# mLSTM, mixture of experts and feed-forward in one kernel: who makes the low parts of w2, how q is laid out, and when x and the first weights arrive

## The chip, the core and the metric

The kernel runs on one core of a Trainium2 chip. The metric is the device time of one execution in microseconds (us): the median of three runs.

## The reference

Three stages follow one another. The first runs over 768 steps, the second sends every token to one of eight experts, the third is a feed-forward net with a PReLU.

```python
for t in range(S):                       # 2 batches x 8 heads, S = 768, head size 40
    m_new = np.maximum(f_gate[:, :, t] + m, i_gate[:, :, t])
    ...
    C = f_stab * C + i_stab * einsum('bhd,bhe->bhde', vt, kt)
    n = f_stab * n + i_stab * kt
    y[:, :, t] = sigmoid(o_gate) * (C @ qt) / max(|n . qt|, 1)
x = y as (1536 tokens, 320)
# experts: 8, capacity 384, 320 -> 1024 -> 320, top 1, weighted by the gate's probability
h = np.maximum(np.einsum('ecd,edf->ecf', disp, w1), 0.0)
out[i] = gate_w[i] * np.einsum('ecf,efd->ecd', h, w2)[expert_idx[i], pos[i]]
# feed-forward: 320 -> 2048 -> 320, weights given in float64
h = x @ w_in
y = (max(h, 0) + alpha * min(h, 0)) @ w_out
```

(Shortened, with the shapes as comments.)

## The kernel before, in words

**mLSTM.** The 1536 tokens are 12 chunks of 128, six for each batch, and line 715 loops over them. A chunk needs a decay matrix `Gb` (GpSimd sets its upper triangle, line 378; ScalarE takes its exponentials), scores of q against k on TensorE (line 393, its moving operand `qbd` is q laid out block-diagonally: three heads share 120 rows, and a head's own 40 rows stand in that head's columns, zeros elsewhere), their product with the decay on VectorE (`Pt`), values (line 456), the state's update (`Ups`, line 427, from `kw`, which GpSimd makes of `tk`, line 402), and a gated output (`rs` on GpSimd, line 492; `xt` on VectorE, line 499). Finished rows are scattered to `disp`, a table of expert slots in DRAM, by an indirect DMA from GpSimd (line 639). Inputs come two chunks at a time: `load_pair` (line 254) loads k and q (`qk`), the block-diagonal q by three DMAs into one of two `qbd` tiles (line 264), and values and keys with tokens as rows (`tk`, line 271). A table of numbers (line 97) says when the loads that don't belong to a chunk are issued: in chunks Z1 to Z1+3 the four quarters of expert 0's weights are loaded by `load_quarter` (line 177: w1 256 KB, its last rows 64 KB, w2 320 KB).

**Experts.** All products are in float32 with each operand split in a high and a low part. Layer 1 of an expert is eight steps f of 128 hidden columns, each eight matmuls of 256 slots (line 938); layer 2 for step f comes two steps later (`LAG`), three matmuls of 320 columns for each of two blocks of 128 slots (lines 950 to 952). A third block of slots runs only if it holds tokens (a run-time If, line 1169); here it does in two experts. Between the layers ScalarE makes `gh` (line 1072) and VectorE `gl` (line 1073). While expert e runs, the weights of expert e+1 are split into high and low parts, a half quarter a step: in even steps w1 (`split1`: ScalarE copies the high part `w1h`; VectorE makes the low part `w1l` and the last rows' low part, a 64x256 "shift" into `w1h`, line 188), in odd steps w2 (`split2`, line 222: ScalarE copies `w2h`, GpSimd makes `w2l`, 128x640). VectorE's part of `split1` is put on a list (`shifts`) that `low_rows` (line 190) empties in the next, odd step, behind that step's `gl` and x. The raw tile is then free and the load for expert e+2 goes out (line 1141). In three steps from XE on the next expert's x is transposed by TensorE and split. VectorE also converts a few tiles of the FFN's weights from float64 (`cv`, lines 976 to 981, five steps for each tile), as many steps as the tuple SC has at each f. When an expert's last accumulation is done, `finish` (line 1157) copies its two blocks, one on VectorE and one on ScalarE (line 1161), and stores them.

**FFN.** Four passes over quarters of the 2048 hidden columns; the first runs over four groups of 2, 2, 4 and 4 blocks of 128 tokens, the others over three groups of four blocks. A step has eight matmuls of 512 columns (layer 1), two passes of ScalarE (`ng`, `g`), VectorE's PReLU (line 1316), the split of g (`g3h` on ScalarE, `g3l` on VectorE, into one of three pairs `ghl3`), and layer 2 two steps later (line 1348). In the first pass the tokens of a group are transposed by TensorE (line 924) and split during the group before: the table XG gives the step for each of the three parts k; a group's layer 1 uses part 0, then part 2, then part 1. The tiles of the last group's x are named `w1h`, `w1l`, `w2h` and `w2l` like the expert tiles whose place they take.

**Order.** TensorE, ScalarE, VectorE and GpSimd run in the order in which the code is written; a queue stands still while its first instruction waits. The DMAs on SyncE's queue are put in order by the scheduler, and some are tied by `after` to an instruction (`anchor[i]`, the last of chunk i's `Pt`), so that they aren't issued ahead of it.

Of the kernel before, what the change touches and what calls it, by code (L numbers as in the profile page):

```python
# [53 lines left out]
def kernel(  # L54
# [177 lines left out]
    with ExitStack() as actx:  # L232
# [16 lines left out]
        for x in range(2):  # L249
            qbds.append(ap.tile([P, 3 * NG, PB], F32, tag=f"qbd{x}", name=f"qbd{x}"))  # L250
            nc.gpsimd.memset(qbds[x], 0.0)
        ins, sgs = {}, {}

        def load_pair(i2, anchor=None, late=None):
# [460 lines left out]
        for i in range(LB):  # L715
# [378 lines left out]
    def expert(e):  # L1094
# [200 lines left out]
    for np0, gi in [(0, g) for g in range(len(FIRST))] + [(p, g) for p in (1, 2, 3) for g in range(len(OTHERS))]:  # L1295
# [4 lines left out]
        for f in range(f0, f1):  # L1300
# [129 lines left out]
```

## Time and profile before

| | |
|---|---|
| median of three runs | 506.01 us (502.34, 506.01, 509.98) |
| profiled execution | 504.48 us, span 502.7 us |
| mean granted TensorE clock in it | 0.925 of full speed |
| busy: TensorE, VectorE, ScalarE, GpSimd | 454.7, 342.4, 246.3, 125.5 us |
| HBM read, written | 56.49 MB, 11.85 MB |

The profile is one execution. TensorE is busy 90% of the span, so what can be won lies in its gaps and in stretches at a lower granted clock. The 40 slices of the page put the slow ones (granted clock below nine tenths) in the mLSTM (to 125 us, with the routing that follows it), and single ones later; the experts run from about 125 to 303 us, the FFN to the end. "Idle before" names what ended an engine's wait; `DVEq` or `PEq` as a releaser is that engine's own sequencer, here at the branch of the If.

### The profile page before, as it was taken

To read this page: it belongs to the slowest core of one execution; us is meant where nothing else is said; L and a number is where in the kernel's file an instruction comes from. 1 tells how busy PE (TensorE), PEld (TensorE's weight loads), DVE (VectorE), ACT (ScalarE), POOL (GpSimd) and SP (SyncE) were. 2 spreads that over 40 slices of the span, in tenths; PEclk is the share of its full clock that TensorE was granted. 3 is DMA by queue.
4 is the path that set the end of the run, shared out by engine and by line. 5 is a ranking of instruction groups with operands and counts; after the bars stand their busy time and mean duration, and the time that the engine had idled before them with its cause. 6 is when DMAs were issued, how large, how long until landed. Compare 5 with 4: busy or idle time off the path is not lost. (4 is left out here: it accounts for less than half of the span.)

```text
span 502.7 us, 8039 instructions
## 1 busy us (share of the span) xinstructions
PE 454.7 (90%) x2800; PEld 408.0 (81%) x2800; DVE 342.4 (68%) x700; ACT 246.3 (49%) x558; POOL 125.5 (25%) x115
## 2 busy tenths in 40 slices
PE   5969998889879889796998898997999999999996
PEld 2658886787879889796998897895998898789995
DVE  7627683866788783859688224775889988764544
ACT  3446782525457544555556124562654454354442
POOL 4244325646534221423233224300000000000000
PEclk8759995966999999889899999997999999999999
DMA  6999999424786753657473003221221231000102
GB/s 190 263 278 337 351 317 253 147 78 133 241 254 197 222 175 88 212 155 244 147 220 94 22 1 103 74 84 42 73 59 53 57 101 52 2 0 1 52 20 86
DMA packets 42428, 68.86 MB, mean 137 GB/s; under 512 B 4383, under 2 KB 32354, under 8 KB 42383
## 3 DMA queue, kind: packets, MB, share of 16 engines
q1 hardware_dynamic: 41023, 64.18, 42.5%
q0 software_dynamic: 1152, 3.86, 2.4%
q8 instruction: 26, 0.43, 0.4%
q10 hardware_dynamic: 208, 0.24, 0.1%
q14 instruction: 19, 0.16, 0.1%
HBM read 56.49 MB, written 11.85 MB: 136 GB/s over the span
## 5 line engine op out<-in xcount | busy, mean ns | idle before, releaser
L188 POOL TENSOR_TENSOR w2l<-w2r,w2h 128x640 fp32r<-128x640 f32 x31 | 53.2, 1715 | 93.1 <-ACT w2h L224 77.8
L1316 DVE SCALAR_TENSOR_TENSOR g<-ng,nalt,g 128x512 f32<-128x512 f32 (+1 forms) x52 | 36.9, 709 | 47.5 <-ACT g L1315 47.4
L1314 ACT ACTIVATE ng<-hps 128x512 f32<-128x512 f32 (+1 forms) x52 | 29.4, 565 | 74.8 <-PE hps L938 73.3
L950 PE MATMUL acc<-w2h,gh 128*128 128x320 f32 x128 | 40.8, 319 | 4.9 <-DVEq L1169 4.9
L952 PE MATMUL acc<-w2h,gl 128*128 128x320 f32 x128 | 40.5, 316 | 1.6 <-DVE gl L1073 1.6
L951 PE MATMUL acc<-w2l,gh 128*128 128x320 f32 x128 | 40.4, 315 | 0.0
L1072 ACT ACTIVATE gh<-hps 128x256 fp32r<-128x256 f32 x50 | 19.1, 384 | 40.3 <-PE hps L938 38.5
L387 ACT ACTIVATE Gb<-Gb,bT 128x128 f32<-128x128 f32 x96 | 29.5, 388 | 12.3 <-POOL Gb L379 12.3
L188 DVE TENSOR_TENSOR w1h<-w1r,w1h 64x256 fp32r<-64x256 f32 x32 | 33.4, 1047 | 1.0
L188 DVE TENSOR_TENSOR g3l<-g,g3h 128x512 fp32r<-128x512 f32 (+1 forms) x52 | 33.5, 644 | 0.1
L1073 DVE SCALAR_TENSOR_TENSOR gl<-hps,gh 128x256 fp32r<-128x256 f32 x50 | 20.5, 421 | 18.6 <-ACT gh L1072 18.1
L952 PE MATMUL acc<-w2h,g3l 128*128 128x320 f32 x96 | 30.3, 316 | 2.4 <-DVE g3l L188 2.3
L952 PE MATMUL acc<-wouth,g3l 128*128 128x320 f32 x96 | 30.8, 321 | 0.3 <-DVE g3l L188 0.3
L950 PE MATMUL acc<-wouth,g3h 128*128 128x320 f32 x96 | 30.7, 320 | 0.1
L1319 ACT CAST g3h<-g 128x512 fp32r<-128x512 f32 (+1 forms) x52 | 30.6, 589 | 0.3 <-DVE g L1316 0.3
L951 PE MATMUL acc<-woutl,g3h 128*128 128x320 f32 x96 | 30.6, 319 | 0.0
L950 PE MATMUL acc<-w2h,g3h 128*128 128x320 f32 x96 | 29.8, 310 | 0.8 <-ACT g3h L1319 0.8
L456 PEld LDWEIGHTS Ops<-tk,Pt 128*128 128x128 f32 x192 | 26.7, 217 | 4.2 <-issue 2.6
L393 PE MATMUL qs<-qbd,qk 120*128 120x384 f32 (+1 forms) x72 | 30.1, 567 | 0.0
L951 PE MATMUL acc<-w2l,g3h 128*128 128x320 f32 x96 | 29.6, 309 | 0.0
L950 PEld LDWEIGHTS acc<-w2h,gh 128*128 128x128 f32 x128 | 25.1, 196 | 5.4 <-issue 3.8
L1315 ACT ACTIVATE g<-hps 128x512 f32<-128x512 f32 (+1 forms) x52 | 29.2, 561 | 0.0
(334 smaller groups left out, 1384.0 us busy)
## 6 DMA issues: line engine op xcount, KB each, us to landing
w2r<-w SPq DMA_DIRECT2D x32, 320.0 KB
w1r<-w SPq DMA_DIRECT2D x32, 256.0 KB
Gb<-gd SPq DMA_DIRECT2D x12, 512.0 KB
raw<-wout SPq DMA_DIRECT2D x8, 640.0 KB
raw<-win SPq DMA_DIRECT2D x8, 512.0 KB
tk<-tok SPq DMA_DIRECT2D x6, 648.0 KB
disp<-zt SPq DMA_DIRECT2D x4, 960.0 KB
qk<-qks SPq DMA_DIRECT2D x5, 720.0 KB
```

What stands on the lines that cost most here:

```text
L188: eng.tensor_tensor(out=out, in0=a, in1=b.bitcast(F32), op=ALU.subtract)
L387: nc.scalar.activation(Dt[i][:, h, :], Dt[i][:, h, :], AF.Exp, bias=bT[:, c, b * H + h:b * H + h + 1])
L393: nc.tensor.matmul(ps[:, :nh * P].rearrange("p (h t) -> p h t", h=nh), kst[:nh * D, g, :], qbd[:nh * D, h0:h0 + nh, :], start=True, stop=True,
L456: nc.tensor.matmul(Opss[i][:, h, :], Pts[i][:, h, :], v1t[:, h, :], start=True, stop=True)
L950: nc.tensor.matmul(a, gh[:, ms], wh, start=first, stop=False)
L951: nc.tensor.matmul(a, gh[:, ms], wl, start=False, stop=False)
L952: nc.tensor.matmul(a, gl[:, ms], wh, start=False, stop=last)
L1073: nc.vector.scalar_tensor_tensor(out=gl, in0=ps, scalar=0.0, in1=gh.bitcast(F32), op0=ALU.max, op1=ALU.subtract)
L1314: nc.scalar.activation(ng, ps, AF.Relu, scale=-1.0)
L1315: nc.scalar.activation(g, ps, AF.Relu)
L1316: nc.vector.scalar_tensor_tensor(out=g, in0=ng, scalar=nalt[:, f:f + 1], in1=g, op0=ALU.mult, op1=ALU.add)
L1319: nc.scalar.copy(gh, g)
```

## The change

**a.** In `split2` the low part of w2 can be made by VectorE, and in the experts always is: it goes on the list `shifts`, and `low_rows` now runs at every step, so that `w2l` stands in an even step and `w1l` with its shift in an odd one, behind the step's `gl` and x. Before, 28 of these ran on GpSimd in the experts, for experts 1 to 7.
**b.** The load that refills the raw quarter is issued one step later.
**c.** Both copies of `finish` go to ScalarE.
**d.** XE goes from 2 to 3, and the conversion steps of SC from f = 0, 5, 7 to f = 0, 2, 6.
**e.** For pairs 1 to 5 the block-diagonal q isn't loaded: `spread_q` makes it of `qk`, multiplying by a column `bd` that is one on a head's 40 rows and zero elsewhere: two products on GpSimd and one on ScalarE for each pair. The three DMAs of each of these pairs (320 KB) are gone, and the clearing of the second `qbd` tile.
**f.** Z1 goes from 6 to 7, and only two quarters of expert 0 are loaded in the loop over chunks, the other two behind it.
**g.** The x tiles `xq` become one slab, whose place is used in the FFN as a fourth pair of `ghl3`; layer 2 then follows three steps behind layer 1.
**h.** XG: the parts of the last group's x in the first pass are transposed at steps 0, 1, 2 instead of 1, 2, 3.

```diff
-    W1, W2, V7, V8, V9, NA, WA, WB, Z0, Z1, X0, LD, FL, XE, SC, SC0, F0, WC, LS, UO, DL, XG, LV, E0, S0, CUT = 12, 4, 0, (((0, 0, 0, 0), (1, 1, 1, 1), (2, 2, 2, 2), (2, 2, 2, 2)), ((1, 2, 2, 3), (1, 2, 2, 3), (1, 2, 2, 3)), ((1, 2, 2, 3), (1, 2, 2, 3), (0, 0, 0, 0)), ((0, 0, 0, 0), (0, 0, 0, 0), (0, 0, 0, 0))), ({0: (2, 3), 1: (4, 5), 2: (6, 7)}, {0: (8, 9), 1: (10, 11)}, {}), 6, 0, 6, 3, 6, 3, 3, (2, 1, 2, 4, 1), 2, (1, 0, 0, 0, 0, 1, 0, 1), (0, 0, 0, 0, 0, 0, 1, 1), {5: [0], 6: [1], 7: [2]}, 0, 1, 1, 4, ({2: (0, 2), 3: (1,)}, {1: (0,), 2: (2,), 3: (1,)}, {1: (0,), 2: (2,), 3: (1,)}), 3, 2, 0, (2, 3, 3, 3, 3, 3, 3, 0)
+    W1, W2, V7, V8, V9, NA, WA, WB, Z0, Z1, X0, LD, FL, XE, SC, SC0, F0, WC, LS, UO, DL, XG, LV, E0, S0, CUT = 12, 4, 0, (((0, 0, 0, 0), (1, 1, 1, 1), (2, 2, 2, 2), (2, 2, 2, 2)), ((1, 2, 2, 3), (1, 2, 2, 3), (1, 2, 2, 3)), ((1, 2, 2, 3), (1, 2, 2, 3), (0, 0, 0, 0)), ((0, 0, 0, 0), (0, 0, 0, 0), (0, 0, 0, 0))), ({0: (2, 3), 1: (4, 5), 2: (6, 7)}, {0: (8, 9), 1: (10, 11)}, {}), 6, 0, 6, 3, 7, 3, 3, (2, 1, 2, 4, 1), 3, (1, 0, 1, 0, 0, 0, 1, 0), (0, 0, 0, 0, 0, 0, 1, 1), {5: [0], 6: [1], 7: [2]}, 0, 1, 1, 4, ({2: (0, 2), 3: (1,)}, {1: (0,), 2: (2,), 3: (1,)}, {0: (0,), 1: (2,), 2: (1,)}), 3, 2, 0, (2, 3, 3, 3, 3, 3, 3, 0)
...
     def split2(e, q, eng=nc.gpsimd, copy=nc.scalar.copy):
         hi, lo = ring2[(NQ * e + q) % RING]
         copy(hi, raw2[q])
-        less(lo, raw2[q], hi, eng)
+        if eng is None:
+            shifts.append(lambda: less(lo, raw2[q], hi, nc.vector))
+        else:
+            less(lo, raw2[q], hi, eng)
...
-            nc.gpsimd.memset(qbds[x], 0.0)
-        ins, sgs = {}, {}
+        nc.gpsimd.memset(qbds[0], 0.0)
+        ins, sgs, q_of = {}, {}, {}
+
+        def spread_q(i2):
+
+            qbd = qbds[i2 % 2][:3 * D].rearrange("p (g j) s -> p g j s", j=3)
+            for j in range(3):
+                n = 3 if j < 2 else 2
+                if j < 2:
+                    nc.gpsimd.tensor_scalar_mul(qbd[:, :n, j, :], q_of[i2][:, :n, :], bd[:, j:j + 1])
+                else:
+                    nc.scalar.activation(qbd[:, :n, j, :], q_of[i2][:, :n, :], AF.Copy, scale=bd[:, j:j + 1])
...
-            for j in range(3):
+            q_of[i2] = qk[:, 0]
+            for j in range(3 if i2 == 0 else 0):
...
-            if Z1 <= i < Z1 + NQ:
+            if Z1 <= i < Z1 + 2:
                 load_quarter(0, i - Z1, anchor[i - 1])
...
             if i % 2 and i // 2 + 2 < NTB // 2:
                 load_pair(i // 2 + 2)
+            if i % 2 == 0 and i // 2 + 1 < NTB // 2:
+                spread_q(i // 2 + 1)
...
+        for q in range(2, NQ):
+            load_quarter(0, q, anchor[i - 1])
         logits(i - 2)
...
             en, (q, fo) = at // NF, divmod(at % NF, 2)
+            low_rows()
             if NF <= at < NF * E:
-                low_rows()
-                (split2(en, q) if fo else split1(en, q, None))
-                if fo and en + 1 < E:
-                    load_quarter(en + 1, q)
+                (split2 if fo else split1)(en, q, None)
+
+                if not fo and at >= NF + 2:
+                    el, ql = divmod(at // 2 - 1, NQ)
+                    if el + 1 < E:
+                        load_quarter(el + 1, ql)
...
-                (nc.scalar.copy if m % 2 else nc.vector.tensor_copy)(ysb[:, m, :], accs[m][:, :DM])
+                nc.scalar.copy(ysb[:, m, :], accs[m][:, :DM])
...
+    ghl3.append([xqs[:, i * GN:(i + 1) * GN] for i in range(2)])
...
-            while len(pend) > LAG:
+            while len(pend) > len(ghl3) - 1:
                 pend.pop(0)()
```

Line numbers of the change are 15 to 24 higher than those of before from the mLSTM on.

**SyncE's queue in the mLSTM**, from the load of the fourth pair's `tk` (pair 3) to that of the fifth (pair 4), before:

```order
L271 DMA tk<-tok 128x1296
L734 DMA disp<-zt 128x6x320
L374 DMA Gb<-gd 128x1024
L264 DMA qbd_134<-qks 40x2x256
L264 DMA qbd_134<-qks 40x3x256 x2
L258 DMA qk<-qks 120x6x256
L734 DMA disp<-zt 128x6x320
L179 DMA w1r_93<-w 128x2x256
L180 DMA w1r_93<-w1t 64x256
L181 DMA w2r_95<-w 128x640
L374 DMA Gb<-gd 128x1024
L271 DMA tk<-tok 128x1296
```

and in the change:

```order
L286 DMA tk<-tok 128x1296
L749 DMA disp<-zt 128x6x320
L389 DMA Gb<-gd 128x1024
L273 DMA qk<-qks 120x6x256
L749 DMA disp<-zt 128x6x320
L389 DMA Gb<-gd 128x1024
L286 DMA tk<-tok 128x1296
```

The three loads of a `qbd` tile and the first quarter of expert 0 (`w1r` twice, `w2r`) no longer stand between the two.

**GpSimd's queue at the same place**, before:

```order
L402 TENSOR_TENSOR kw<-tk,Gb 128x320
L379 AFFINE_SELECT Gb<-Gb 128x1024
L492 TENSOR_TENSOR rs<-sg_161,rec 128x320
L402 TENSOR_TENSOR kw<-tk,Gb 128x320
L379 AFFINE_SELECT Gb<-Gb 128x1024
L492 TENSOR_TENSOR rs<-sg_408,rec 128x320
L402 TENSOR_TENSOR kw<-tk,Gb 128x320
```

and in the change, where L265 is `spread_q` for the fifth pair, in chunk 6:

```order
L417 TENSOR_TENSOR kw<-tk,Gb 128x320
L394 AFFINE_SELECT Gb<-Gb 128x1024
L507 TENSOR_TENSOR rs<-sg_155,rec 128x320
L417 TENSOR_TENSOR kw<-tk,Gb 128x320
L265 TENSOR_SCALAR qbd_129<-qk,ct 120x3x256 x2
L394 AFFINE_SELECT Gb<-Gb 128x1024
L507 TENSOR_TENSOR rs<-sg_399,rec 128x320
L417 TENSOR_TENSOR kw<-tk,Gb 128x320
```

The two products of `spread_q` now stand between a `kw` and the next `Gb`, ahead of the next `rs`.

**VectorE's queue in an expert** (three steps of the same expert; `gl` begins a step), before:

```order
L1073 SCALAR_TENSOR_TENSOR gl_1423<-hps_1430,gh_1422 128x256
L188 TENSOR_TENSOR x11l<-qs_71,x11h 128x384
L188 TENSOR_TENSOR w1l_1376<-w1r_93,w1h_1366 128x512
L188 TENSOR_TENSOR w1h_1366<-w1r_93,w1h_1366 64x256
L1073 SCALAR_TENSOR_TENSOR gl_1419<-hps_1431,gh_1418 128x256
L188 TENSOR_TENSOR x12l<-qs_70,x12h 64x384
L1073 SCALAR_TENSOR_TENSOR gl_1421<-qs_72,gh_1420 128x256
L188 TENSOR_TENSOR w1l_1378<-w1r_93,w1h_1368 128x512
L188 TENSOR_TENSOR w1h_1368<-w1r_93,w1h_1368 64x256
```

and in the change:

```order
L1092 SCALAR_TENSOR_TENSOR gl_1413<-hps_1425,gh_1412 128x256
L190 TENSOR_TENSOR x11l<-qs_71,x11h 128x384
L190 TENSOR_TENSOR w2l_1371<-w2r_90,w2h_1361 128x640
L1092 SCALAR_TENSOR_TENSOR gl_1415<-qs_72,gh_1414 128x256
L190 TENSOR_TENSOR x12l<-qs_70,x12h 64x384
L190 TENSOR_TENSOR w1l_1372<-w1r_88,w1h_1362 128x512
L190 TENSOR_TENSOR w1h_1362<-w1r_88,w1h_1362 64x256
L1092 SCALAR_TENSOR_TENSOR gl_1417<-hps_1424,gh_1416 128x256
L190 TENSOR_TENSOR w2l_1373<-w2r_91,w2h_1363 128x640
```

Each odd step still has `w1l` and the shift (`w1h`, 64x256) behind its `gl`, and each even step now has a `w2l` of its own, ahead of the next step's `gl`.

**TensorE's queue in the FFN's first pass**, where the third part of the last group's x is transposed (L924), before:

```order
L950 MATMUL acc<-wouth_1390,g3h_3861 128x320
L951 MATMUL acc<-woutl_1391,g3h_3861 128x320
L952 MATMUL acc<-wouth_1390,g3l_3862 128x320
L924 MATMUL xtp<-ct,sums 128x128 x4
L938 MATMUL hps<-w1h_1370,winh_1388 128x512
L938 MATMUL hps<-w1l_1380,winh_1388 128x512
L938 MATMUL hps<-w1h_1370,winl_1389 128x512
L938 MATMUL hps<-w1h_1372,winh_1388 128x512
```

and in the change (L943):

```order
L971 MATMUL acc<-wouth_1388,xq 128x320
L943 MATMUL xtp<-ct,sums 128x128 x4
L957 MATMUL hps<-w1h_1360,winh_1386 128x512
L957 MATMUL hps<-w1l_1370,winh_1386 128x512
L957 MATMUL hps<-w1h_1360,winl_1387 128x512
L957 MATMUL hps<-w1h_1362,winh_1386 128x512
L957 MATMUL hps<-w1l_1372,winh_1386 128x512
L957 MATMUL hps<-w2h_1361,winh_1386 128x512
L957 MATMUL hps<-w2l_1371,winh_1386 128x512
L957 MATMUL hps<-w2h_1361,winl_1387 128x512
L969 MATMUL acc<-wouth_1384,g3h_3855 128x320
L970 MATMUL acc<-woutl_1385,g3h_3855 128x320
```

Before, the last group's layer 1 follows the transposition at once; in the change a step of layer 1 of the group ahead, and a layer 2 of four blocks (twelve matmuls, of which the last two rows are the first), stand between them.

## Rows read from the trace of the kernel before

**Rows 1.** Timeline, GpSimd (start, us, line op, [idle before and its releaser]), mLSTM loop.

```profile
32.32 0.72 POOL L492 TENSOR_TENSOR rs<-sg,rec 128x320 f32<-128x320 f32 x1 [0.61 <-DVE rec L487]
...
44.99 0.72 POOL L492 TENSOR_TENSOR rs<-sg,rec 128x320 f32<-128x320 f32 x1 [2.42 <-PE Ups L427]
...
58.66 0.72 POOL L492 TENSOR_TENSOR rs<-sg,rec 128x320 f32<-128x320 f32 x1 [5.98 <-DVE eqv L558]
...
69.69 0.72 POOL L492 TENSOR_TENSOR rs<-sg,rec 128x320 f32<-128x320 f32 x1 [2.69 <-DVE rec L487]
76.93 0.73 POOL L402 TENSOR_TENSOR kw<-tk,Gb 128x320 f32<-128x320 f32 x1 [6.52 <-DMA tk<-tok]
...
89.42 0.72 POOL L492 TENSOR_TENSOR rs<-sg,rec 128x320 f32<-128x320 f32 x1 [5.54 <-PE Ips L418]
```

**Rows 2.** Timeline, TensorE (same columns; x is the count of a merged row), mLSTM loop.

```profile
77.72 1.45 PE L427 MATMUL Ups<-tk,kw 128*120 128x123 f32 x6 [3.15 <-POOL kw L402]
```

**Rows 3.** Windows: start:end, length, busy PE, PEld, DVE, ACT, POOL; granted clock; DMA share, GB/s.

```profile
60.00:77.00 17.00, 14.56 (x114) 13.12 (x112) 13.63 (x48) 12.95 (x40) 5.05 (x7) 0.99 1.02 314
78.00:90.00 12.00, 12.00 (x48) 10.53 (x48) 5.16 (x16) 3.92 (x14) 6.25 (x7) 0.50 1.02 264
125.00:303.50 178.50, 159.70 (x1172) 153.90 (x1170) 123.58 (x215) 87.80 (x183) 59.64 (x43) 0.97 0.53 161
210.00:218.00 8.00, 7.30 (x33) 7.06 (x34) 4.10 (x10) 1.92 (x4) 0.00 (x0) 0.59 0.36 105
240.00:244.00 4.00, 4.00 (x23) 3.95 (x21) 0.98 (x2) 1.59 (x3) 0.00 (x0) 0.57 0.55 168
344.00:350.00 6.00, 6.00 (x19) 5.48 (x20) 3.18 (x4) 1.59 (x3) 0.00 (x0) 0.52 0.00 0
```

**Rows 4.** Lines by form, GpSimd, whole span: names, shapes, count, busy us, mean ns, idle.

```profile
L188 POOL TENSOR_TENSOR w2l<-w2r,w2h 128x640 fp32r<-128x640 f32 x31 | 53.2, 1715 | 93.1 <-ACT w2h L224 77.8 <-PE hps L938 11.2 <-issue 4.1
L379 POOL TENSOR_SCALAR_AFFINE_SELECT Gb<-Gb 128x1024 f32<-128x1024 f32 x12 | 13.9, 1160 | 19.5 <-DMA Gb<-gd 19.5
...
L595 POOL TENSOR_SCALAR spots<-zt,sf 128x384 fp32r<-128x384 f32 x1 | 1.3, 1283 | 1.4 <-DVE mv L561 1.4
...
L790 POOL TENSOR_SCALAR nalt<-alt 128x16 f32<-128x16 f32 x1 | 0.5, 497 | 0.0
```

**Rows 5.** Waits, 125 to 303.5: engine and line, releaser, us in total, times, longest.

```profile
PE hps L938 <- DVE gl L1073: 7.9, 8, 2.9
...
PE acc L950 <- DVEq L1169: 4.9, 2, 3.5
```

**Rows 6.** Lines by form, VectorE, 125 to 303.5 (columns as in the fourth group).

```profile
L188 DVE TENSOR_TENSOR w1h<-w1r,w1h 64x256 fp32r<-64x256 f32 x30 | 32.6, 1089 | 0.9
L188 DVE TENSOR_TENSOR w1l<-w1r,w1h 128x512 fp32r<-128x512 f32 x28 | 24.9, 888 | 1.0 <-DVEq L1169 0.8
...
L1161 DVE COPY held_rows<-acc 128x320 f32<-128x320 f32 x7 | 3.4, 482 | 0.0
...
L188 DVE TENSOR_TENSOR woutl<-cv,wouth 128x640 fp32r<-128x640 f32 x2 | 1.6, 820 | 0.0
```

**Rows 7.** Timeline, VectorE, experts 1 and 5 (columns as in the first group).

```profile
149.14 0.42 DVE L188 TENSOR_TENSOR w1h<-w1r,w1h 64x256 fp32r<-64x256 f32 x1
...
154.53 1.68 DVE L188 TENSOR_TENSOR w1h<-w1r,w1h 64x256 fp32r<-64x256 f32 x1
...
238.46 0.48 DVE L1161 COPY held_rows<-acc 128x320 f32<-128x320 f32 x1
```

**Rows 8.** Timeline, GpSimd, expert 1.

```profile
154.02 1.91 POOL L188 TENSOR_TENSOR w2l<-w2r,w2h 128x640 fp32r<-128x640 f32 x1 [3.04 <-ACT w2h L224]
```

**Rows 9.** Timeline, TensorE, FFN, first pass, before its last group.

```profile
340.56 0.50 PE L938 MATMUL hps<-w2h,winh 128*128 128x512 f32 x1 [0.72 <-ACT w2h L200]
343.95 0.80 PE L938 MATMUL hps<-w2l,winh 128*128 128x512 f32 x1 [2.89 <-DVE w2l L188]
```

**Rows 10.** Waits, 303.5 to 500 (columns as in the fifth group).

```profile
PE acc L952 <- DVE g3l L188: 2.6, 6, 0.9
```

More of the change, by code (lines that the diff above doesn't have):

```diff
@@ L141, in x_tiles @@
         return t
-    xq = x_tiles(xk, SL, 0)
+    xqs = xk.tile([P, 6 * SL], F32R, name="xq")
+    xq = [[xqs[:, (2 * k + i) * SL:(2 * k + i + 1) * SL] for i in range(2)] for k in range(3)]
+    nc.gpsimd.memset(xq[2][1][r:].bitcast(U32), 0)
     RING = 2 * NQ
@@ L267, in load_pair @@
                 )
-                if i2 < 2:
-                    after(d, anchor)
+                after(d, anchor)
             tk = rp.tile([P, 2, tok.shape[2]], F32, tag="tk", name="tk")
```

## The prediction

> **What bounds the kernel now.** I read the page's 40 slices first, then the waits and windows of each of the three stages, then the timelines around the longest waits. TensorE is busy for 90% of the span and no other engine comes near, so time is won only where TensorE waits, or where it works at the lower of its clock levels. Such places are in all three stages.
>
> *mLSTM.* GpSimd's `kw` at 76.93 stood 6.52 us behind the load of `tk` [rows 1], and TensorE's `Ups` then 3.15 us behind `kw` [rows 2]. From 60 to 77 the granted clock was 0.99; in the twelve microseconds from 78 on it was 0.50, which is 1.2 instead of 2.4 GHz, while TensorE was busy throughout [rows 3]. Twelve microseconds at half speed hold work for six. The stall and its aftermath thus cost 3.15 + 6.0 = 9.2 us. In both stretches the DMA engines were busy all the time, at 314 and 264 GB/s [rows 3]: `tk` was late because other loads stood ahead of it.
>
> *Experts.* In the 178.5 us TensorE was busy 159.7, VectorE 123.6, GpSimd 59.6 [rows 3]: on average nothing else is a bound. But TensorE waited 7.9 us in eight places for `gl` and 4.9 us in two at the branch of the If, behind VectorE [rows 5]. At the second of these VectorE did its copy for `finish` only at 238.46 [rows 7]. After two long waits the clock was low: 0.59 over 8 us and 0.57 over 4 [rows 3], a loss of 8 x 0.41 + 4 x 0.43 = 5.0 us. Together 12.8 + 5.0 = 17.8 us. VectorE is late because some of its work is slow: the 64x256 shift took 0.42 us at 149.14 and 1.68 at 154.53 [rows 7], the latter while GpSimd ran its `w2l` from 154.02 for 1.91 us [rows 8]. The mean over 30 is 1089 ns, 32.6 us in all [rows 6].
>
> *FFN.* Before the last group of the first pass TensorE waited 0.72 and 2.89 us for the parts of the group's x [rows 9], and the clock was 0.52 over the next 6 us [rows 3], which loses 6 x 0.48 = 2.9. Together 6.5 us. Waits of layer 2 for `g3l` are another 2.6 us, spread over six places [rows 10].
>
> **The change, part by part.**
>
> *The low parts of w2 (a, b).* VectorE gets 28 operations of 128x640 with both inputs in SBUF. The nearest row is its own `woutl` of that form, 820 ns [rows 6]: 28 x 0.82 = 23.0 us. If the shifts fall to the 0.42 us that they take alone, VectorE saves 30 x (1.089 - 0.42) = 20.1 us, and 3.4 us more with the seven copies that go to ScalarE [rows 6]. Its busy time becomes 123.6 + 23.0 - 20.1 - 3.4 = 123 us, as much as before; what falls is the size of its lumps (a `w2l` one step, `w1l` and shift the next). The other slow forms that could recover, `w1l` at a mean of 888 ns among them [rows 6], I leave as a reserve. The bounds: 0.82 us at best for `w2l`, and at worst the 1.715 us that GpSimd's takes [rows 4]. I take 0.82, since that row is the same engine and form. The raw w2 tile is read until a step later and its refill goes out a step later, out of six or seven steps between load and use; the DMA share of 0.53 [rows 3] covers that.
>
> The Trainium skill, "SBUF — State Buffer", section "Who interferes with whom", says that a VectorE instruction with two SBUF inputs contends with a GpSimd instruction that reads SBUF, and that the loser stands still for the whole of it; the trace agrees (0.42 against 1.68 us). By that rule the 20.1 us come back in full.
>
> *Copies, x and conversions (c, d).* ScalarE takes seven copies in its 87.8 us of 178.5 [rows 3]; idle time hides them. The branch then no longer stands behind a VectorE copy. XE and SC only spread VectorE's work: three conversion steps an expert as before, all in steps that hold a `w2l`, where there is no shift. Price nothing; if the cover fails it is one `gl` late by a conversion.
>
> Of the 17.8 us I take 14: a wait for `gl` can come back where a conversion, x and `w2l` meet, and after the If in two experts.
>
> *q (e) and the first weights (f).* Ahead of the late `tk` the queue loses four pairs' block-diagonal loads of 320 KB and one quarter of 640 KB, 1.92 MB: 6.1 us at 314 GB/s, 7.3 us at 264. That is as much as the wait of 6.52, so `kw` comes on time or nearly. The last pair's `tk` gains 1.6 + 0.64 MB. The two quarters that move behind the loop are used after it, where the page's DMA line falls below half: nothing.
>
> `spread_q` adds two GpSimd operations and one of ScalarE to each of five pairs. No row has GpSimd's form (120x768, one input, a scalar by partition). Low bound: the triangle's 1160 ns for 1024 columns [rows 4] gives 0.87 us for 768. High bound: a TENSOR_SCALAR of 384 columns, 1283 ns [rows 4], doubled, 2.57. The same operation with 16 columns takes 497 ns [rows 4]; the line through both gives 2.1 at 768, which I take, as it is the same kind of instruction. A pair then costs GpSimd 4.2 us. These stand ahead of the `rs` that before began at 32.32, 44.99, 58.66, 69.69 and 89.42, after idle times of 0.61, 2.42, 5.98, 2.69 and 5.54 us [rows 1]. What doesn't fit is 3.6 + 1.8 + 0 + 1.5 + 0 = 6.9 us; at 0.87 it is 1.1 and at 2.57 it is 9.7. Behind each spread wait the next `Gb` and `rs`, and for the first pair the scores themselves; but `rs` feeds `xt` of the chunk before, whose transposition comes late on TensorE, so lateness there doesn't all reach it. I take 2.5 us, a third. The cleared tile (`qbd1`) is saved at the start, behind loads: nothing.
>
> The rule above speaks against this part: `spread_q` reads SBUF on GpSimd for some 4 us a pair, and VectorE's two-input operations would stand still behind it. No run so far shows it for this form; by the shift's rows each one hit would lose up to a microsecond (an estimate), one or two a pair.
>
> mLSTM: -9.2 + 2.5 = -6.7.
>
> *FFN (g, h).* The last group's x is transposed a step earlier; eight matmuls of layer 1 and twelve of layer 2 now lie between its last part and its use. VectorE's backlog there was 2.89 us; the cover is longer than that, since before the step was nothing. I take the whole 6.5 us. A lag of three instead of two takes a part of the 2.6; I count 0.5, because VectorE, which makes `g3l`, gets no faster. FFN: -7.
>
> **Sum.** 504.5 - 6.7 - 14 - 7 = 476.8 us, taken against the profiled execution (504.48, of which 502.7 is the span). That run lies 1.5 us under the median, inside the spread of the three; I don't correct for it. Forecast 477.
>
> **Rivals.**
> - *The shifts stay slow* (not GpSimd's reading but something of their own makes them so). VectorE then has 123.6 + 23.0 - 3.4 = 143 us, lumps as late as now, and the experts gain nothing: 504.5 - 13.7 = 490.8. Against it: the fast and slow shifts lie 5 us apart, with the same operands, and differ in GpSimd [rows 7, 8].
> - *GpSimd becomes what mLSTM waits for.* At 2.57 us an operation 9.7 us are exposed, which eats the 9.2: 504.5 + 0.5 - 21 = 484. For it: GpSimd's queue is in order, and `spread_q` also waits for the `qk` load with `Gb` behind it. Against: two of the five idles are over 5 us [rows 1].
> - *The FFN's wait only moves*: the earlier x takes VectorE's time from the `g3l` of the group that runs, and layer 2 waits instead: FFN 0, 504.5 - 20.7 = 483.8. For it: six waits for `g3l` are there already [rows 10].
> - *The other side: slower.* `w2l` costs VectorE 1.715 us, as it did GpSimd, and the shifts stay at 1.089. VectorE then has 123.6 + 48.0 - 3.4 = 168.2 us, over TensorE's 159.7, and its 44.6 us more lie in every expert's steps. It decides from 13.7 + 10.1 = 23.8 us exposed on, a little over half. With two thirds, 30 us: 504.5 - 13.7 + 30 = 521. Against: 820 ns for the same form [rows 6].
>
> **How the numbers follow.** Forecast 0.70, with its own range of 468 to 487; shifts stay slow 0.10; GpSimd in mLSTM 0.09; FFN's wait moves 0.06; slower 0.05. With every gain in full and the low price of the spread it is 504.5 - 8.1 - 17.8 - 9.1 = 469.5; with some of the reserve in `w1l` 466. The high end takes in the slow shifts, 491. What 2% of 506 us, 10.1 us, doesn't tell from no change lies between 496 and 516. The forecast and the first three rivals are all below; two of them failing together, or only part of the slow case, come to lie within: faster 0.90, same 0.06, slower 0.04.
>
> **What would show it.** Right: shifts near 0.42 us throughout from expert 1 on and GpSimd idle there; `w2l` on VectorE near 0.82; no wait of `kw` for `tk` in chunk 8 and a granted clock near 1 after 78 us; no wait over 1 us at the If's branch; no wait at the last group's first layer 1. Wrong: shifts above 1 us without GpSimd; waits for `spread_q` in the scores or in `rs`; a new low clock elsewhere, which would give the gains back.

## The result, and the profile after

The change took the median from 506.01 to 477.23 us (475.65 to 480.26); the ratio is 0.9475, 95% interval 0.9338 to 0.9612. The profiled execution took 477.23 us, its span 475.4. The runs of one kernel differ with the clock that was granted over the run (before: 500.3 us at a mean of 0.938, 512.9 at 0.913), and two of the profiles below (spread on VectorE, x late) are of longer runs at a lower clock, so ratios of two kernels within 2% of each other say little, and the waits and the stages without their low clock say more.

I mark the stages by TensorE's first layer 1 of expert 0 and of the FFN. For the clock I cut each profile into windows of 2 us and add up (1 - granted clock) x 2 us over those below 0.8 ("low clock"); what is left of a stage without it is its net.

| us | mLSTM | experts | low clock | net | FFN | low clock | net |
|---|---|---|---|---|---|---|---|
| before | 125.3 | 178.2 | 4.7 | 173.6 | 199.2 | 5.1 | 194.1 |
| after | 119.2 | 166.3 | 8.4 | 157.9 | 189.9 | 3.4 | 186.5 |
| difference | -6.0 | -12.0 | +3.7 | -15.7 | -9.3 | -1.7 | -7.6 |

**mLSTM.** GpSimd's timeline after (start, us, line and operation, count, idle before it and what ended that):

```profile
27.55 4.39 POOL L265 TENSOR_SCALAR qbd<-qk,ct 120x768 f32<-120x768 f32 x2
...
66.69 4.63 POOL L265 TENSOR_SCALAR qbd<-qk,ct 120x768 f32<-120x768 f32 x2
...
73.02 0.73 POOL L417 TENSOR_TENSOR kw<-tk,Gb 128x320 f32<-128x320 f32 x1
```

The `kw` that waited 6.52 us for `tk` [rows 1] follows `rs` at once, without a wait. In its place stands the spread, 4.39 and 4.63 us a pair (2.29 us an operation over all ten). TensorE's scores of chunks 2, 4 and 8, in its timeline, wait for it:

```profile
32.00 3.78 PE L408 MATMUL qs<-qbd,qk 120*128 120x384 f32 x6 [2.92 <-POOL qbd L265]
...
46.22 1.99 PE L408 MATMUL qs<-qbd,qk 120*128 120x384 f32 x6 [0.96 <-POOL qbd L265]
...
71.38 1.99 PE L408 MATMUL qs<-qbd,qk 120*128 120x384 f32 x6 [0.64 <-POOL qbd L265]
```

These are 4.5 us; they fall on the three pairs for which GpSimd's idle time before had been too short [rows 1]. The longest of them stands in the place of another wait. Before, the same scores began at 31.96, behind a wait of `Ups` for `kw` of chunk 1:

```profile
30.72 1.45 PE L427 MATMUL Ups<-tk,kw 128*120 128x123 f32 x6 [4.15 <-POOL kw L402]
```

Here 0.25 us of it are left. GpSimd waits for the load of chunk 1's `Gb`, and without the loads of q that comes some 3 us sooner: GpSimd starts on it at 25.78 instead of 28.87 (25.29 to 26.69 in all eleven profiles that don't load q for pairs 1 to 5, 28.67 to 29.83 in the three that do). The spread takes this back: the scores of chunk 2 begin at 31.5 to 32.9 us in all nine profiles that have it on GpSimd, at 31.8 to 32.9 in the three that load q.

In the windows (busy TensorE, its weight loads, VectorE, ScalarE, GpSimd; granted clock; DMA share; GB/s) the clock from 78 to 90, 0.50 before [rows 3], is 0.86 (1.00 until it falls at 84):

```profile
78.00:90.00 12.00, 10.86 (x71) 9.24 (x70) 8.30 (x32) 5.47 (x18) 10.71 (x10) 0.86 0.56 169
119.23:285.52 166.29, 161.32 (x1171) 157.26 (x1170) 113.08 (x236) 90.31 (x190) 11.48 (x15) 0.95 0.56 173
176.00:190.00 14.00, 14.00 (x64) 14.00 (x64) 2.49 (x7) 2.08 (x7) 0.00 (x0) 0.51 0.00 1
```

**Experts.** The second row above is the whole stage. VectorE is busy 113.1 us (123.6 before, over 178.5 us [rows 3]), GpSimd 11.5. VectorE's lines of the stage (count, busy us, mean ns, idle before):

```profile
L190 DVE TENSOR_TENSOR w2l<-w2r,w2h 128x640 fp32r<-128x640 f32 x28 | 22.8, 816 | 0.0
...
L190 DVE TENSOR_TENSOR w1l<-w1r,w1h 128x512 fp32r<-128x512 f32 x28 | 19.1, 682 | 0.8 <-DVEq L1191 0.5
L190 DVE TENSOR_TENSOR w1h<-w1r,w1h 64x256 fp32r<-64x256 f32 x30 | 13.6, 455 | 0.9
```

The shift is at 455 ns (1089 before), `w1l` at 682 (888), and `w2l` at 816, near the 820 of `woutl` [rows 6]. TensorE's waits for VectorE (total, times, longest) were 12.8 us [rows 5] and are:

```profile
PE qs L957 <- DVE gol L1092: 0.9, 1, 0.9
PE hps L957 <- DVE gl L1092: 0.9, 1, 0.9
```

The wait at the branch of the If is gone. But the third row of the windows is new: 14 us at 0.51 in the run-time block of expert 2, though TensorE was busy throughout. It gives back 6.8 us of what was won. Before, the same block ran at a clock of 1.00 (183.5 to 197 us).

**FFN.** Ahead of the last group of the first pass TensorE waits 0.82 us instead of 0.72 and 2.89 [rows 9], and the clock doesn't fall behind it (1.00 from 309 to 318):

```profile
309.14 0.50 PE L957 MATMUL hps<-w2l,winh 128*128 128x512 f32 x1 [0.82 <-DVE w2l L190]
```

### The profile page after: what moved, and what is told of

It reads as the page before. It is cut to its first block, busy times and chain, and to the rows that moved or that the text cites. A ratio compares the mean times of both kernels' runs of the same rounds, so it can differ in the third digit from the quotient of the medians.

```text
span 475.4 us, 7953 instructions
## 1 busy us (share of the span) xinstructions
PE 449.0 (94%) x2800; PEld 407.5 (86%) x2800; DVE 330.2 (69%) x721; ACT 252.7 (53%) x570; POOL 98.1 (21%) x96
## 5 line engine op out<-in xcount | busy, mean ns | idle before, releaser
L408 PE MATMUL qs<-qbd,qk 120*128 120x384 f32 (+1 forms) x72 | 28.9, 546 | 7.0 <-POOL qbd L265 4.5
L1091 ACT ACTIVATE gh<-hps 128x256 fp32r<-128x256 f32 x50 | 19.1, 383 | 29.3 <-PE hps L957 28.9
L1092 DVE SCALAR_TENSOR_TENSOR gl<-hps,gh 128x256 fp32r<-128x256 f32 x50 | 21.0, 421 | 12.8 <-ACT gh L1091 12.2
L408 PEld LDWEIGHTS qs<-qbd,qk 120*128 120x128 f32 (+1 forms) x72 | 15.3, 228 | 16.6 <-POOL qbd L265 5.1
L1339 ACT ACTIVATE g<-hps 128x512 f32<-128x512 f32 (+1 forms) x52 | 29.2, 561 | 0.0
L471 PE MATMUL Ops<-tk,Pt 128*128 128x41 f32 x192 | 26.4, 303 | 0.7 <-DVE Um L458 0.7
L209 ACT CAST w1h<-w1r 128x768 fp32r<-128x768 f32 x31 | 25.8, 831 | 0.0
L190 DVE TENSOR_TENSOR g3l<-g,g3h 128x512 fp32r<-128x512 f32 (+1 forms) x39 | 25.1, 643 | 0.0
L971 PEld LDWEIGHTS acc<-w2h,gl 128*128 128x128 f32 x128 | 24.3, 190 | 0.8 <-DVE gl L1092 0.5
L957 PE MATMUL hps<-xq,w1h 128*128 128x256 f32 x144 | 24.7, 287 | 0.0
L970 PEld LDWEIGHTS acc<-w2l,gh 128*128 128x128 f32 x128 | 24.6, 192 | 0.0
L190 DVE TENSOR_TENSOR w2l<-w2r,w2h 128x640 fp32r<-128x640 f32 x29 | 23.7, 816 | 0.0
L226 ACT CAST w2h<-w2r 128x640 fp32r<-128x640 f32 x31 | 22.6, 728 | 1.8 <-ACTq L1191 1.0
```

Source lines behind the costliest of these rows:

```text
L190: eng.tensor_tensor(out=out, in0=a, in1=b.bitcast(F32), op=ALU.subtract)
L209: copy(hi, a)
L408: nc.tensor.matmul(ps[:, :nh * P].rearrange("p (h t) -> p h t", h=nh), kst[:nh * D, g, :], qbd[:nh * D, h0:h0 + nh, :], start=True, stop=True,
L471: nc.tensor.matmul(Opss[i][:, h, :], Pts[i][:, h, :], v1t[:, h, :], start=True, stop=True)
L957: nc.tensor.matmul(ps, a, b_, start=j == 0 and 0 in ks, stop=j == len(seq) - 1 and 1 in ks)
L970: nc.tensor.matmul(a, gh[:, ms], wl, start=False, stop=False)
```

## The experiments

All kernels but the second start from the changed kernel. Where several kernels share a stage's code, their nets agree within 2 us (experts: 157.9, 157.8, 157.5, 158.4 and 159.4; FFN: 186.0 to 187.9), so parts of 3 us and more can be told. The mLSTM can't be read so finely: eight profiles with the changed code there end it between 117.2 and 126.8 us (mean 120.6), with 14.9 to 29.2 us of low clock; the two with the code of before (the kernel before and the second one here) end it at 125.3 and 125.4, with 26.1 and 23.4.

| kernel | median us | ratio to before, 95% | mLSTM | experts (net) | FFN (net) |
|---|---|---|---|---|---|
| w2 low parts on GpSimd | 479.06 | 0.9478 (0.9345, 0.9611) | 122.8 | 168.2 (168.2) | 187.4 (187.4) |
| before + w2 low parts on VectorE | 498.24 | 0.9860 (0.9734, 0.9985) | 125.4 | 174.2 (165.0) | 197.0 (196.0) |
| GpSimd also reads | 498.56 | 0.9841 (0.9695, 0.9987) | 126.8 | 183.2 (175.0) | 188.8 (187.8) |
| GpSimd also writes | 472.69, 487.92 | none | 119.0 | 162.4 (159.1) | 189.5 (186.5) |
| q loaded | 478.73 | 0.9506 (0.9397, 0.9614) | 122.7 | 164.5 (157.8) | 188.5 (186.9) |
| quarters early | 471.76 | 0.9358 (0.9192, 0.9523) | 118.5 | 157.5 (157.5) | 188.8 (187.2) |
| spread on VectorE | 473.64 | 0.9286 (0.9077, 0.9494) | 119.3 | 166.7 (158.4) | 189.5 (186.0) |
| x late in the FFN | 488.16 | none | 117.6 | 167.5 (159.4) | 196.8 (190.4) |
| one copy on VectorE | 487.19 | 0.9653 (0.9551, 0.9755) | 120.3 | 170.7 (162.5) | 188.9 (187.9) |
| x and conversions as before | 473.04 | 0.9428 (0.9345, 0.9512) | 122.1 | 164.3 (163.3) | 189.4 (186.0) |
| third bank | 476.14 | 0.9445 (0.9353, 0.9536) | 117.2 | 168.3 (165.1) | 187.7 (187.7) |
| spread on VectorE, third bank | 474.59 | 0.9439 (0.9374, 0.9503) | 115.2 | 169.7 (165.3) | 188.6 (187.0) |

**The low parts of w2, undone and alone.**

```diff
-                (split2 if fo else split1)(en, q, None)
+                (split2(en, q) if fo else split1(en, q, None))
```

> The changed kernel with the low parts of w2 in the experts back on GpSimd, the rest as changed. Experts' stage (first layer 1 of expert 0 to the FFN's first layer 1): 178.3 us before, 166.3 after the change. Theory (GpSimd's reading makes VectorE's shifts slow, and late VectorE makes TensorE wait): mean of the 64x256 shifts in the experts back from 0.45 to about 1.0 us, the stage 173 to 180 us, total 484 to 491 us. Rival (the copies on ScalarE and the new places of x and conversions brought the gain): shifts may be slow, but the stage stays at 166 to 169 and the total at 477 to 480.

The second kernel is the one before with `split2`, `low_rows` and the loads of the experts as in the change, and nothing else.

> The kernel before with one part of the change alone: the low parts of w2 on VectorE, a step later, and the loads a step later. Theory: shifts near 0.42 us, the experts' stage falls from 178.3 to 166 to 170 us, total 493 to 498 us; mLSTM and FFN as before. Rival (copies, x and conversions are what counts): stage 174 to 178, total above 500.

Undone, the shifts are slow again, and TensorE waits for VectorE in twelve places:

```profile
L190 DVE TENSOR_TENSOR w1h<-w1r,w1h 64x256 fp32r<-64x256 f32 x30 | 31.4, 1048 | 0.9
```

```profile
PE hps L957 <- DVE gl L1092: 6.8, 9, 1.5
...
PE acc L971 <- DVE gl L1092: 2.5, 2, 1.6
...
PE acc L971 <- DVEq L1191: 0.6, 1, 0.6
```

That is 9.9 us, and the stage's net is 10.3 us longer than after the change. Its raw length is only 1.9 us longer, because the clock never fell in this profile:

```profile
122.84:291.01 168.17, 155.76 (x1171) 149.32 (x1170) 122.90 (x208) 90.17 (x190) 58.95 (x42) 1.00 0.57 170
```

Hence a stage and a median (479.06) in the rival's range, which alone would say that this part is worth nothing. Alone on the kernel before, the part brings the shifts to 455 ns, as in the change, and takes 8.6 us off the net; with 9.2 us of low clock the raw stage, 174.2, is in the rival's range here too. It leaves the wait at the branch (4.7 us in two places):

```profile
PE acc L953 <- DVEq L1175: 4.7, 2, 2.8
...
PE hps L941 <- DVE gl L1076: 2.1, 2, 1.2
```

Both theories hold for a part: the low parts of w2 bring 8.6 us of net alone and 10.3 with the other edits there, the other edits alone 5.4 (173.6 - 168.2).

**What makes the shifts slow.** In the two kernels GpSimd is given work again at each `w2h`, after a ScalarE copy of one element that holds it back (`scr` and `tiny` are new tiles that nothing needs):

```diff
                 (split2 if fo else split1)(en, q, None)
+                if fo:
+                    nc.scalar.copy(tiny, scr[:, 0, :1])
+                    less(scr, raw2[q], ring2[(NQ * en + q) % RING][0], nc.gpsimd)
```

> The changed kernel; in each step that makes a high part of w2 GpSimd also computes the same difference once more into a tile that nobody uses (28 times, two inputs in SBUF), after a copy of one element on ScalarE. Theory (reading on GpSimd blocks VectorE's two-input operations): shift, w1l or w2l on VectorE slow by about 1 us where they meet it, VectorE's busy time in the stage up by 15 to 30 us, stage 170 to 185, total 481 to 495. Rival (VectorE's slow shifts had another cause): shifts 0.42 to 0.5, total 477 to 480.

In the other, the last line is three times `nc.gpsimd.memset(scr, 0.0)`.

> As the run with the second difference, but GpSimd clears the unused tile three times (128x640 each, about 0.64 us, no input) in its place, after the same copy of one element on ScalarE. Theory (it is reading that blocks): shifts 0.42 to 0.5 us as in the changed kernel, total 477 to 480. Rival (any work on GpSimd blocks, as it holds the way to SBUF): shifts near 1 us, VectorE's busy time up by 10 us and more, total 481 to 495.

VectorE's lines from 119 to 305 us, with reads and then with writes:

```profile
L190 DVE TENSOR_TENSOR w2l<-w2r,w2h 128x640 fp32r<-128x640 f32 x29 | 32.1, 1107 | 0.0
L190 DVE TENSOR_TENSOR w1h<-w1r,w1h 64x256 fp32r<-64x256 f32 x32 | 31.0, 972 | 1.0
L190 DVE TENSOR_TENSOR w1l<-w1r,w1h 128x512 fp32r<-128x512 f32 x29 | 22.3, 769 | 0.9 <-DVEq L1197 0.4
```

```profile
L190 DVE TENSOR_TENSOR w2l<-w2r,w2h 128x640 fp32r<-128x640 f32 x28 | 22.8, 814 | 0.0
...
L190 DVE TENSOR_TENSOR w1h<-w1r,w1h 64x256 fp32r<-64x256 f32 x30 | 12.5, 419 | 0.9
```

One place of each, with reads VectorE and then GpSimd:

```profile
160.60 1.69 DVE L190 TENSOR_TENSOR w1h<-w1r,w1h 64x256 fp32r<-64x256 f32 x1
...
163.73 1.73 DVE L190 TENSOR_TENSOR w1l<-w1r,w1h 128x512 fp32r<-128x512 f32 x1
165.49 0.42 DVE L190 TENSOR_TENSOR w1h<-w1r,w1h 64x256 fp32r<-64x256 f32 x1
```

```profile
160.31 1.70 POOL L190 TENSOR_TENSOR scr<-w2r,w2h 128x640 f32<-128x640 f32 x1 [3.11 <-ACT tiny L1165]
163.04 1.87 POOL L190 TENSOR_TENSOR scr<-w2r,w2h 128x640 f32<-128x640 f32 x1 [1.03 <-ACT tiny L1165]
```

and with writes:

```profile
151.65 0.42 DVE L190 TENSOR_TENSOR w1h<-w1r,w1h 64x256 fp32r<-64x256 f32 x1
...
152.44 0.82 DVE L190 TENSOR_TENSOR w2l<-w2r,w2h 128x640 fp32r<-128x640 f32 x1
```

```profile
151.34 2.02 POOL L1167 MEMSET scr<- 128x640 f32 x3 [2.92 <-ACT tiny L1165]
```

With reads, a VectorE operation that starts after GpSimd's ends only some 0.3 to 0.6 us after it: the shift at 160.60 ends at 162.29, GpSimd at 162.01; `w1l` at 163.73 takes 1.73 instead of 0.68 us and ends at 165.46, GpSimd at 164.91; the next shift, clear of it, takes 0.42. With writes a shift that lies wholly beside them takes 0.42. Both kinds write the same tile, so it is not GpSimd's being at work that blocks, nor its writing, but the operation that reads two tiles; in these places an operation of VectorE loses the rest of it. (Not every GpSimd operation that reads does this: see the last section.) The net of the stage grows by 17.1 us with reads, by 1.2 with writes. This is what the Trainium skill, "SBUF — State Buffer", section "Who interferes with whom", states for VectorE with two SBUF inputs, and these runs agree.

**q and the first quarters.** First q loaded again (`spread_q` not called, the three DMAs for every pair and both `qbd` tiles cleared):

```diff
-            for j in range(3 if i2 == 0 else 0):
+            for j in range(3):
```

> The changed kernel with the block-diagonal q of pairs 1 to 5 loaded again, two quarters of expert 0 still behind the loop. mLSTM stage (start to the first layer 1 of expert 0): 125.3 us before, 119.2 after the change. Theory (bytes ahead of tk made kw late, and the spread on GpSimd costs less than the wait): kw of chunk 8 waits 2 to 5 us for tk again, stage 122 to 126, total 480 to 484 us. Rival (the spread's 4.5 us of TensorE waits eat what the bytes give, the two quarters alone would do): stage 115 to 119, total 473 to 477.

GpSimd's timeline, and TensorE's:

```profile
28.67 1.09 POOL L396 TENSOR_SCALAR_AFFINE_SELECT Gb<-Gb 128x1024 f32<-128x1024 f32 x1 [8.75 <-DMA Gb<-gd]
...
74.85 0.74 POOL L419 TENSOR_TENSOR kw<-tk,Gb 128x320 f32<-128x320 f32 x1 [2.52 <-ACT Gb L404]
...
91.48 0.74 POOL L419 TENSOR_TENSOR kw<-tk,Gb 128x320 f32<-128x320 f32 x1 [3.44 <-DMA tk<-tok]
```

```profile
30.52 1.45 PE L444 MATMUL Ups<-tk,kw 128*120 128x123 f32 x6 [5.77 <-POOL kw L419]
```

The theory's sign did not come: `kw` of chunk 8 (74.85) waits for ScalarE's `Gb` and not for `tk`. A wait for `tk`, 3.4 us, stands only before the `kw` of chunk 10, and no wait of TensorE's behind it. The loaded q costs at the start instead: `Gb` of chunk 1 comes as late as before, and TensorE waits 5.8 us for the `kw` behind it. The stage ends at 122.7, inside what the changed code also shows; the ratio differs from the change's by 0.003, so no gain of the spread in time is shown. Then the quarters:

```diff
-            if Z1 <= i < Z1 + 2:
+            if Z1 <= i < Z1 + NQ:
```

(with Z1 6 and without the loads behind the loop)

> The changed kernel with the four quarters of expert 0 loaded in chunks 6 to 9 again, q still spread on chip. Theory: 640 KB more ahead of tk of pairs 4 and 5, about 2 us later each, of which the bytes saved by the spread hide most: stage 119 to 122, total 477 to 480. Rival (it was the quarters that made tk late): kw waits over 4 us, stage 123 to 126, total 481 to 485.

```profile
POOL kw L417 <- DMA tk<-tok: 0.2, 1, 0.2
```

All four quarters fit: `kw` of chunk 8 waits 0.2 us, and the stage ends at 118.5. So either part alone takes away the 6.52 us: the quarters' move with q loaded, the spread with the quarters early. With q spread, moving them back had brought nothing. Its median of 471.76 owes most to the clock: no low window lies in its experts.

Nor does that wait always cost what I read from the profile before. The second kernel has the mLSTM of before, and its `kw` of chunk 8 is as late. But TensorE comes to its `Ups` later there (granted clock 0.80 from 60 to 77, 0.99 in the kernel before) and doesn't wait, and the clock stays at 1.00 until 86; GpSimd, and then TensorE:

```profile
77.58 0.74 POOL L405 TENSOR_TENSOR kw<-tk,Gb 128x320 f32<-128x320 f32 x1 [6.76 <-DMA tk<-tok]
```

```profile
78.37 0.83 PE L430 MATMUL Ups<-tk,kw 128*120 128x123 f32 x6
```

Its stage ends at 125.4 all the same. So no run shows that the stall of chunk 8 and the fall behind it are what the change gained; which part shortens the stage stays open. Last, the spread's products on VectorE:

```diff
-                    nc.gpsimd.tensor_scalar_mul(qbd[:, :n, j, :], q_of[i2][:, :n, :], bd[:, j:j + 1])
+                    nc.vector.tensor_scalar_mul(qbd[:, :n, j, :], q_of[i2][:, :n, :], bd[:, j:j + 1])
```

> The changed kernel with the two products of spread_q that GpSimd made on VectorE. GpSimd's took 2.29 us each, and TensorE waited 2.92, 0.96 and 0.64 us for them. Theory: VectorE needs 0.5 to 0.7 us each (its one-input conversion steps of 128x768 take 0.55), TensorE's waits for qbd fall below 1 us in all, stage 114 to 117, total 471 to 475. Rival (VectorE's own queue is what mLSTM waits for next): stage 118 to 121, total 476 to 479.

```profile
L265 DVE TENSOR_SCALAR qbd<-qk,ct 120x768 f32<-120x768 f32 x10 | 9.6, 1003 | 1.8 <-DMA qk<-qks 1.8
```

VectorE needs 1.00 us, more than the 0.5 to 0.7 expected, and TensorE no longer waits for `qbd`: the scores of chunk 2 begin at 28.53 instead of 32.00. But they do so behind a wait for `kw`, whose `Gb` is still awaited from its load:

```profile
27.29 1.45 PE L442 MATMUL Ups<-tk,kw 128*120 128x123 f32 x6 [3.31 <-POOL kw L417]
```

The stage's end, 119.3, shows no gain (the low clock in it is 23.6 us against the change's 21.4), and the ratio's interval overlaps the change's. Not settled by this run alone.

**The FFN.**

```diff
-{0: (0,), 1: (2,), 2: (1,)}), 3, 2, 0,
+{1: (0,), 2: (2,), 3: (1,)}), 3, 2, 0,
```

(the end of the table's line, the rest unchanged)

> The changed kernel with the parts of the last group's x in the FFN's first pass at steps 1, 2, 3 again. FFN stage 199.2 us before, 189.9 after the change. Theory: TensorE waits 3 to 4 us before the last group and the clock falls for some 6 us: stage 195 to 197, total 482 to 485. Rival (the lag of three gave the FFN's gain): wait back, but stage 190 to 192 and total 477 to 479.

```profile
323.24 0.50 PE L957 MATMUL hps<-w2h,winh 128*128 128x512 f32 x1 [0.82 <-ACT w2h L202]
326.63 0.79 PE L957 MATMUL hps<-w2l,winh 128*128 128x512 f32 x1 [2.89 <-DVE w2l L190]
```

Both waits are back, to the hundredth of the longer one, and 3.0 us of low clock behind them. The net is 3.9 us longer, the stage 6.9 us. The 3.0 are not fixed: behind the same wait of 2.89 us the second kernel has 1.0. The runs (474.15, 483.68, 492.64 and one of 706.48 at a mean granted clock of 0.549) spread too widely for a ratio.

**Copies, x and conversions.**

```diff
-                nc.scalar.copy(ysb[:, m, :], accs[m][:, :DM])
+                (nc.scalar.copy if m % 2 else nc.vector.tensor_copy)(ysb[:, m, :], accs[m][:, :DM])
```

> The changed kernel with one of the two copies of finish back on VectorE (7 copies). With w2's low parts back on GpSimd the stage was 168.2 us, so the copies and the new places of x and conversions hold most of the experts' gain; this run and that with the old places tell which. If the copies matter: TensorE waits at the branch of the If again for 2 us and more in sum (4.9 before, 4.7 with w2's part alone, none after the change), total 480 to 484 us. If the new places matter: under 1 us there, total 476 to 479.

```profile
PE acc L969 <- DVEq L1191: 4.6, 2, 2.7
```

The wait at the branch is back as it was, and the net grows by 4.6 us.

```diff
-... 3, (1, 0, 1, 0, 0, 0, 1, 0), ...
+... 2, (1, 0, 0, 0, 0, 1, 0, 1), ...
```

> The changed kernel with XE and SC as before (x of the next expert in steps 2 to 4, conversions in steps 0, 5 and 7). If the new places matter: TensorE waits for gl 3 us and more in sum and at the branch again (experts 3 and 5, where conversions stand in steps 7 and 0, ahead of finish), total 480 to 485 us. If the copies matter: waits under 2 us, total 476 to 479.

```profile
PE hps L957 <- DVE gl L1092: 2.1, 2, 1.2
PE qs L943 <- DVEq L1191: 2.1, 2, 1.5
...
PE acc L971 <- DVE gl L1092: 1.6, 1, 1.6
```

Waits of 5.8 us in five places, net +5.4. So both matter, and by nearly as much. Undone one at a time, the low parts, the copies and the places lose 10.3 + 4.6 + 5.4 = 20.3 us, more than the 15.7 that all gained: so the parts overlap, and none of these numbers is a part's share. The median of 473.04 hides it: its low clock in the experts is 1.0 us against 8.4.

**The clock in the run-time block.**

```diff
-        hb = xps if more else hps[:2]
+        hb = xps + hps[2:] if more else hps[:2]
```

> The changed kernel with a third PSUM bank for the run-time block's layer 1 (before two). In the changed kernel's profile TensorE waited 0.94 us for gol in that block of expert 2, and the granted clock was near 0.5 over the next 14 us, which lost 6.8 us; four of the other runs show the same fall and three don't, with the same wait. Theory (the wait starts the fall): wait gone, no fall in that block, stage 160 to 163, total 470 to 474. Rival (the fall comes of that block's sparse work or of what went before): wait gone, fall still there, total 475 to 479.

Without the edit, seven of twelve profiles (that of the change among them) show the fall in the block of expert 2, five don't. The kernel with the early quarters has the same wait of 0.9 us in it, and runs it like this:

```profile
169.00:183.00 14.00, 13.05 (x107) 12.91 (x106) 6.54 (x24) 4.46 (x14) 0.00 (x0) 1.00 0.16 54
```

With the third bank the wait is gone, and neither of its two profiles shows a fall. But by five in twelve, two in two can be chance. And the bank, which the steps outside the block use too, brings a new wait at the branch, which eats it:

```profile
PE qs L957 <- DVEq L1191: 8.2, 5, 3.8
```

And both, the bank and the spread's products on VectorE:

> The third bank together with the two products of spread_q on VectorE. On VectorE they took 1.00 us each instead of 2.29 and TensorE's waits for qbd went (473.6 us with that alone). If the two add: total 467 to 471 us. If the third bank gives nothing: 472 to 476, as with the products on VectorE alone.

The two together end the mLSTM earliest, at 115.2, and pay the same at the branch (8.0 us). None of the variants with a lower ratio can be told from the change: their intervals overlap 0.9338 to 0.9612.

## Why the prediction was right, point by point

- **The sum** held: -27.7 forecast, -27.3 measured between the two profiled spans, and 477.23 us against 477. The stages are 0.7 us less (mLSTM), 2.0 less (experts) and 2.3 more (FFN) than their terms. That the whole fits so closely is partly luck, since a fall of the clock is worth up to 7 us.
- **mLSTM.** `kw`'s wait went, and the clock from 78 on was 0.86 instead of 0.50. But the 9.2 us were read from one profile: the second kernel has the same late `kw` with neither TensorE's wait nor the fall behind it, and its stage is as long. The price of the spread was mis-sized: 2.29 us an operation instead of 2.1, and 4.5 us of TensorE's time instead of 2.5; it reached TensorE in the three pairs named, through the scores that need the new tile, not through `rs`. The sum also left out that without the loads of q `Gb` of chunk 1 comes 3 us sooner; the first pair's spread, 2.92 of the 4.5 us, takes only that back, and the scores of chunk 2 begin when they did. The step of the bytes counted both parts as needed; either alone was enough for chunk 8. One profile of this stage is uncertain by some 5 us. Seven of the eight of the changed code end it earlier than both of before, by 4.7 us in the mean over all eight: the sign is confirmed, the prices of the parts are not, and that -6.0 came so close to -6.7 is luck in part.
- **Experts.** The 17.8 us that I saw there were there: net -15.7. I took 14 for waits that might come back, and 3.7 came back as low clock, in a block I hadn't named; "a new low clock elsewhere" stood among the signs of a wrong step. Wrong was the step that priced the new places of x and conversions (d) at nothing: with the old ones and `w2l` on VectorE the waits for `gl` and at the branch return (net +5.4). The copies (c) I counted only through the branch's wait of 4.9; they measured 4.6. VectorE's busy time came out at 113.1 us instead of 123: `w1l` fell from 24.9 to 19.1 us, the reserve that I had left out; the rest is in other operations.
- **FFN.** The one step earlier was worth 3.9 + 3.0 = 6.9 us against 6.5. The longer lag and what else changed there is 3.7 us of net by difference (194.1 - 190.4; 5.6 from the 196.0 of the second kernel, whose FFN is that of before), against 0.5: mis-sized, because I reasoned from the waits for `g3l` alone, 2.6 us, and took a fifth of them, while the change and the kernel with the late x have none left. The lag wasn't tried by itself, so where the rest comes from stays open.
- **The rivals.** Slow shifts of their own making: refuted by reads and writes. GpSimd as the mLSTM's bound: partly so, 4.5 us of waits, without the loss of the whole gain. The FFN's moved wait: 0.82 us remain before the last group, and none for `g3l`. `w2l` at GpSimd's price on VectorE: 816 ns, refuted.

## What to carry to other kernels

An engine far from busy can still be the one that is waited for, if its work comes in lumps; look at the largest lump ahead of each hand-over, and at what another engine does while it runs slow. Judge an edit by the waits and the net length of its stage where the granted clock falls now in one place and now in another: two of the experiments had medians that hid 5 and 10 us of waits. A stall seen in one profile is not yet a price: look in a second profile of the same code whether it costs the same there. When a part is spread over idle time of a queue in order, compare each idle time with the whole of what is put ahead of it, for every occurrence.

## What the runs showed of the hardware that I had not expected

I had expected, from the rule of the Trainium skill cited above and in the prediction, that `spread_q` would block VectorE's two-input operations. It doesn't. VectorE and then GpSimd, in the change's mLSTM:

```profile
57.94 1.01 DVE L499 SCALAR_TENSOR_TENSOR den<-t,den 128x8 f32<-128x8 f32 x1
...
69.34 0.70 DVE L497 TENSOR_SCALAR den<-t 128x8 f32<-128x8 f32 x1
...
81.99 0.49 DVE L514 TENSOR_TENSOR xt<-t,rs 128x320 f32<-128x320 f32 x1 [2.81 <-DMA disp<-xt,si]
```

```profile
57.85 1.08 POOL L394 TENSOR_SCALAR_AFFINE_SELECT Gb<-Gb 128x1024 f32<-128x1024 f32 x1
...
80.37 4.39 POOL L265 TENSOR_SCALAR qbd<-qk,ct 120x768 f32<-120x768 f32 x2
```

`xt`, two inputs in SBUF, took 0.49 us in the middle of a spread (80.37 to 84.76), and so did the one at 53.23 (0.48 us, spread from 53.09 on). But `den`, of 128x8, which takes 0.17 us alone, took 1.01 beside the triangle's selection and ended with it, at 58.95 against 58.93. In the nine profiles with this spread on GpSimd, the 21 `xt` that ran beside the spread alone took 0.48 to 0.57 us, and 23 of 24 of this `den` 0.17 (one 0.68); all twelve `den` beside the selection alone took 1.00 to 1.01. Both GpSimd operations read one tile from SBUF (the product also a column of scalars); the product with a scalar by partition doesn't block VectorE's two-input operations here, the selection does. The sentence of the Trainium skill makes no such difference; the measurement decides. What in the two forms differs wasn't tried. Nor is a spread free for all of VectorE: `den`'s first operation, with one input from SBUF, takes 0.16 us alone and took 0.70 at 69.34, inside the spread of 66.69 to 71.32. What held it isn't shown.

The granted clock fell in the same block, with the same instructions, in seven profiles and not in five others; the wait in it was 0.9 to 1.3 us in the seven and 0.5 to 1.3 in the five. Of the five kernels that have it at 0.9 us, four show the fall. What decides it stays open.
